# Loading k's last rows ahead of q's, and taking k's norms before q's, at the start of an attention-and-feed-forward kernel

## The chip, the cores and the metric

The kernel runs on one core of a Trainium2 chip. The metric is the device time of that core in microseconds (us), lower is better. Before the change it was 720.33 us (median of 3 runs, 720.29 to 720.56).

Each run gives two figures. *Time* is the metric. *Span* is the stretch from the first to the last thing that the profile of that run shows. The time is 1.7 to 2.9 us longer than the span, and that difference wanders from run to run without the kernel having a part in it. Where tenths of a microsecond matter, the span is the sharper of the two, and I give both. Each run also has a mean granted TensorE clock, 1.000 being full speed.

## The reference

```python
# B, N, C = 4, 6080, 256
qn = q / (norm(q, axis=1) + 1e-6)           # norms over the 6080 rows, one per channel
kn = k / (norm(k, axis=1) + 1e-6)
s  = kn.transpose(0, 2, 1) @ qn / tau       # 256 x 256 scores per batch, tau = 1
a  = softmax(s, axis=-1)
x  = (v @ a).reshape(B * N, C)
h  = relu(x @ w_in)                         # 256 -> 2048
out = (s_moe * h * h + b_moe) @ w_out       # 2048 -> 256
```

Nothing of the feed-forward part can begin before the first batch's softmax is known, and that needs the sums of squares over all 6080 rows of k and q. So the last rows to arrive stand at the head of a chain: square, norm, root, scaling, exp, fold into w_in, first product.

## The kernel before

The names: PE is TensorE (matmuls), ACT is ScalarE, DVE is VectorE, POOL is GpSimd, which issues the loads. Batch 0 is read in 13 pieces. The first eleven hold 4 rows per partition, the last two 2 rows per partition, on 128 and on 96 partitions. In the text, q11 and q12 are q's last two pieces, k11 and k12 those of k.

```python
def load(self, c):
    ...
    for i, src in enumerate((k, q)):                       # k's piece, then q's piece
        ...
        po(nc.gpsimd.dma_start(out=t[:np_, i, :jc, :], in_=rows))

for c in range(NDIRECT, len(g0.chunks)):
    g0.load(c)                                             # ... k11, q11, k12, q12, then w_in, v
```

`po` keeps the order of the program on an engine. The scores of a piece are the `mm` matmuls; `keep_busy` issues matmuls whose result nobody reads, to keep PE's clock up.

```python
for c in range(NCH0):
    ops = g0.norm_ops(c)              # square of k on ACT, of q on DVE, folds on DVE
    if c >= NCH0 - 3:
        g0.add_norms()                # matmuls with ones: sums of squares of earlier pieces
    for j in range(g0.chunks[c][2]):
        g0.mm(c, j)                   # scores
    fill = FILL.get(c - NCH0, 0)      # 4 for the piece before the last two, 1 behind piece 11
    if fill:
        keep_busy(fill, ...)
    for f in ops:
        f()

fin = g0.finish_ops()
fin[1]()   # norms of k and q together on PE, one root on ACT
fin[2]()   # + eps and reciprocal on DVE, of k and q
fin[3]()   # scores times 1/|k| on DVE
fin[4]()   # ready(Exp): loads ACT's table for exp, with a tiny exp called warm
keep_busy(4, w_in16[:, 0, :P], w_in16[:, 0, :NW])
fin[5]()   # turn: four transposes of the scores on PE
transpose_v(0)
for f in fin[6:12]:
    f()    # exps, sums, folds into w_in
```

After that the main loop runs in steps: a step has one first product (`mm1`, two matmuls of 512 columns), one relu on ACT every second step, and second products. Those of group 0 are placed by one line:

```python
if s == gp * FT + PLAG[gp] + (mp * 3 // 2 if gp == 0 else mp):     # FT = 16, PLAG[0] = 11
    plain_mm2(gp, mp)
```

## Time and profile before

| | before |
|---|---|
| time, median | 720.33 us |
| span of the profiled run | 718.5 us |
| PE busy | 97% of the span |
| q's last rows land | 34.36 us |
| first exp on ACT | 37.36 us |
| group 1's sums S begin on DVE | 68.73 us |
| PE without a stall from | 76 us |

How to read it: PE is full from 76 us to 703, and its work after that is the same in both kernels. So whatever the change gains or loses is decided before 76 us. The lines that carry this are shown and explained in the prediction.

### The profile page before, as it was taken

The numbers are of one execution on the slowest core, as the hardware profiler recorded it, in microseconds if no ns is written. First come the engines' busy times: TensorE is split into PE (matmuls) and PEld (weight loads), VectorE is DVE, ScalarE is ACT, GpSimd is POOL, SyncE is SP. The second block draws the span as 40 slices with busy tenths as digits, with TensorE's granted clock in tenths as the row PEclk, the third lists the DMA queues.
The fourth block names the chain that finished last, engine by engine and source line by source line (L and its number), as shares of the span: only waits on it lengthen the run. The fifth ranks groups of instructions, "written<-read, shape, count | busy, mean of one in ns | idle before, by whom it ended". The sixth has DMA issues, their size and how long they took to land.

```text
span 718.5 us, 17642 instructions
## 1 busy us (share of the span) xinstructions
PE 699.4 (97%) x7481; PEld 505.0 (70%) x7481; DVE 625.9 (87%) x879; ACT 544.5 (76%) x588; POOL 109.8 (15%) x189
## 2 busy tenths in 40 slices
PE   4799999999999999999999999999999999999998
PEld 3556777776677777777677777777668777777777
DVE  4779999998889999999888899999887888888886
ACT  4489877887777777788777777778877777777875
POOL 4532332201201222111110222110000000000000
PEclk9999999999999999999999999999999999999999
DMA  9999999547565979443973777844423333321202
GB/s 237 207 259 148 172 166 149 110 103 134 103 105 120 153 133 144 105 96 75 152 155 63 139 136 125 154 93 83 105 65 75 92 71 74 97 59 46 83 30 75
DMA packets 89791, 84.27 MB, mean 117 GB/s; under 512 B 59664, under 2 KB 64848, under 8 KB 89712
## 3 DMA queue, kind: packets, MB, share of 16 engines
q0 software_dynamic: 26064, 43.40, 37.7%
q1 hardware_dynamic: 63072, 38.43, 21.5%
q8 instruction: 59, 0.97, 0.5%
q10 hardware_dynamic: 576, 1.31, 0.5%
q14 instruction: 20, 0.16, 0.1%
HBM read 78.91 MB, written 24.90 MB: 144 GB/s over the span
## 4 chain that ended last, share of the span: by engine, by line
PE 92%; DMA 4%; ACT 1%; DVE 1%; POOL 0%; issue 0%; ACTq 0%; POOLq 0%
PE h_ps L605 45%; PE o_ps L773 40%; PE s_ps L142 4%; PE wa_ps L309 2%; DMA qk<-in_q_dram 2%; DMA qk<-in_k_dram 1%; DMA w_in<-in_moe_w_in_dram 1%; ACT r L615 1%; PE o_ps L651 0%; POOL qk L126 0%; PE o_ps L677 0%; ACT g L626 0%; PE idle_ps L442 0%; DVE o_sb L633 0%; DVE sq L162 0%
## 5 line engine op out<-in xcount | busy, mean ns | idle before, releaser
L615 ACT ACTIVATE r<-h_ps 128x1024 f16<-128x1024 f32 (+1 forms) x384 | 387.6, 1013 | 146.9 <-PE h_ps L605 145.0
L605 PE MATMUL h_ps<-vT,wa 128*128 128x512 f16 (+7 forms) x1632 | 451.9, 364 | 0.6 <-ACT r L615 0.4
L773 PEld LDWEIGHTS <-S 128*128 128x128 f16 x2944 | 197.9, 98 | 85.1 <-DVE S L699 0.4
L773 PEld LDWEIGHTS <-g 128*128 128x128 f16 x2208 | 155.0, 98 | 74.1
L628 DVE TENSOR_TENSOR g<-r 128x2048 f16<-128x2048 f16 (+2 forms) x150 | 174.7, 1165 | 15.1 <-ACT r L615 14.9
L773 PE MATMUL o_ps<-T,S 128*128 128x128 f16 x2208 | 183.2, 219 | 0.3 <-DVE S L699 0.2
L605 PEld LDWEIGHTS <-wa 128*128 128x128 f16 x1632 | 136.0, 98 | 21.4 <-issue 1.0
L773 PE MATMUL o_ps<-w_out,g 128*128 128x128 f16 x1472 | 134.2, 219 | 0.3 <-DVE u L633 0.3
L633 DVE SCALAR_TENSOR_TENSOR o_sb<-o_ps,s_out,u 128x256 f32<-128x256 f32 x138 | 66.4, 481 | 47.6 <-PE o_ps L773 45.1
L626 ACT ACTIVATE g<-r 128x1024 f16<-128x1024 f16 (+1 forms) x97 | 100.4, 1035 | 0.2
L142 PE MATMUL s_ps<-qk 128*128 128x256 f16 (+1 forms) x384 | 70.0, 283 | 14.0 <-ACT qk L133 8.7
L361 POOL DMA_DIRECT2D v<-in_v_dram x48 | 31.3, 656 | 263.0 <-DMA vT<-v 199.5
L633 DVE SCALAR_TENSOR_TENSOR u<-o_ps,s_out,rowconst 128x256 f32<-128x256 f32 x138 | 65.9, 478 | 0.0
L773 PE MATMUL o_ps<-w_out,S 128*128 128x128 f16 x736 | 63.4, 219 | 0.0
L773 PE MATMUL o_ps<-N,g 128*128 128x128 f16 x736 | 63.4, 219 | 0.0
L188 POOL DMA_DIRECT2D f<-f x30 | 26.3, 877 | 225.8 <-DVE f L178 167.0
L165 ACT ACTIVATE sq<-qk 128x1024 f16<-128x1024 f16 (+3 forms) x49 | 50.4, 1033 | 10.3 <-DMA qk<-in_k_dram 6.3
L701 DVE TENSOR_TENSOR S<-S,g 128x2048 f16<-128x2048 f16 (+1 forms) x47 | 56.4, 1201 | 1.3
L699 DVE TENSOR_TENSOR S<-g 128x2048 f16<-128x2048 f16 (+1 forms) x47 | 56.0, 1192 | 0.0
L705 DVE TENSOR_TENSOR S<-g,S 128x2048 f16<-128x2048 f16 x46 | 55.9, 1216 | 0.0
L703 DVE TENSOR_TENSOR S<-g 128x2048 f16<-128x2048 f16 x46 | 55.9, 1215 | 0.0
L142 PEld LDWEIGHTS <-qk 128*128 128x128 f16 (+1 forms) x384 | 32.9, 101 | 19.8 <-DVE qk L132 8.1
(75 smaller groups left out, 324.3 us busy)
## 6 DMA issues: line engine op xcount, KB each, us to landing
out_dram<-o_sb SPq DMA_DIRECT2D x46, 512.0 KB, 3.0
v<-in_v_dram POOLq DMA_DIRECT2D x47, 256.0 KB, 4.7
qk<-in_k_dram POOLq DMA_DIRECT2D x42, 256.0 KB, 6.0
qk<-in_q_dram POOLq DMA_DIRECT2D x42, 256.0 KB, 7.2
f<-f POOLq DMA_DIRECT2D x30, 128.0 KB, 3.0
vT<-v SPq DMA_TRANSPOSE x182, 3.2
w<-in_moe_w_out_dram POOLq DMA_DIRECT2D x4, 512.0 KB, 11.4
raw<-in_q_dram ACTq DMA_DIRECT2D x2, 512.0 KB, 6.6
```

The lines of the kernel that those rows point to most:

```text
L142: po(nc.tensor.matmul(self.s_ps[:, ch, :], kc[:np_, j, ts(ch, P)], qc[:np_, j, :], start=(c == 0 and j == 0 and ch == 0), stop=(c == len(s ...
L165: po(nc.scalar.activation(out=st["sq"][:np_, 1, js, :], in_=kc[:np_, js, :], func=AF.Square))
L605: po(nc.tensor.matmul(dst, wa[:, ci, ts(m, P)], src, start=(ci == 0), stop=(ci == CH - 1), skip_group_check=True))
L615: po(nc.scalar.activation(out=r16[:, :, i % 2, :n], in_=h_tiles.pop((g, i))[:, :, :n], func=AF.Relu))
L626: po(nc.scalar.activation(out=dst, in_=src, func=AF.Square))
L628: po(nc.vector.tensor_mul(dst, src, src))
L633: po(nc.vector.scalar_tensor_tensor(out=dst, in0=src, scalar=s_out, op0=ALU.mult, in1=add, op1=ALU.add))
L699: po(nc.vector.tensor_add(T[1], A21, A22))
L701: po(nc.vector.tensor_sub(T[2], T[1], A11))
L703: po(nc.vector.tensor_sub(T[3], A11, A21))
L705: po(nc.vector.tensor_sub(T[4], A12, T[2]))
L773: po(nc.tensor.matmul(st[name][:, j, :], a()[:, i, ts(j, P)], w[:, i, :], start=first, stop=last, skip_group_check=True))
```

## The change

The intent: k's last rows are asked for ahead of q's, so that all that depends on k alone (its norms, their roots, their reciprocals, the scaling of the scores) can be done ahead of q's norms. Besides that, three of the four padding matmuls ahead of the transposes go, and group 0's second products are placed at 4/3 of a step instead of 3/2. The diff cut to its core:

```diff
-    for c in range(NDIRECT, len(g0.chunks)):
+    for c in range(NDIRECT, len(g0.chunks) - 2):
         g0.load(c)
+    for parts in ((0,), (1,)):                       # k11, k12, then q11, q12
+        for c in range(len(g0.chunks) - 2, len(g0.chunks)):
+            g0.load(c, parts)
...
+    NFILL = 1
...
+    fin = g0.finish_ops()
     for c in range(NCH0):
         ops = g0.norm_ops(c)
         if c >= NCH0 - 3:
             g0.add_norms()
+        if c == NCH0 - 1:
+            for f in ops:
+                f()
+            fin[0]()                                 # norms of k, and their root
         for j in range(g0.chunks[c][2]):
             g0.mm(c, j)
...
-    fin[1](); fin[2](); fin[3](); fin[4]()           # (four lines in the original)
-    keep_busy(4, w_in16[:, 0, :P], w_in16[:, 0, :NW])
-    fin[5]()
+    for f in fin[1:6]:      # norms of q, ready(Exp), recip of k, scale, recip of q
+        f()
+    keep_busy(NFILL, w_in16[:, 0, :P], w_in16[:, 0, :NW])
+    fin[6]()                # turn
...
-                if s == gp * FT + PLAG[gp] + (mp * 3 // 2 if gp == 0 else mp):
+                if s == gp * FT + PLAG[gp] + (mp * 4 // 3 if gp == 0 else mp):
```

The rest of the diff (cut here) splits the norm tile, the root and the reciprocal into one for k and one for q in batch 0, and leaves the later batches as they were.

More of the change, by code (lines that the diff above doesn't have):

```diff
@@ L114, in __init__, with load @@
             self.tiles = {}
-            self.rows, self.n_ps = [], None
-        def load(self, c):
+            self.raw, self.rows, self.n_ps = {}, ([], []), [None, None]
+        def load(self, c, parts=(0, 1)):
             at, np_, jc = self.chunks[c]
-            t = qk_pool.tile([P, 2, JC, C], FP16, tag="qk", name="qk")
+            if 0 in parts:
+                self.raw[c] = qk_pool.tile([P, 2, JC, C], FP16, tag="qk", name="qk")
+            t = self.raw[c]
             direct = self.b == 0 and c < NDIRECT
-            for i, src in enumerate((k, q)):
+            for i in parts:
+                src = (k, q)[i]
                 rows = src[self.b, at : at + np_ * jc, :].rearrange("(p j) c -> p j c", j=jc)
@@ L181, in f @@
                     if last and (self.b == 0 or c == 0 or c == len(self.chunks) - 1):
-                        self.rows.append((st["f", half], np_, 1))
+                        for rows in self.rows:
+                            rows.append((st["f", half], np_, 1))
                 return f
             def into_first():
-                dst, src = self.rows[0][0][:np_], st["f", 1][:np_]
+                dst, src = self.rows[0][0][0][:np_], st["f", 1][:np_]
                 po(nc.gpsimd.dma_start(out=dst, in_=src, accum_op=ALU.add))
             def unfolded():
-                self.rows.append((st["sq"], np_, jc))
+                for rows in self.rows:
+                    rows.append((st["sq"], np_, jc))
             ops = []
@@ L202, in norm_ops, with add_norms @@
             return ops + [into_first] if self.b > 0 and 0 < c < len(self.chunks) - 1 else ops
-        def add_norms(self, last=False):
-            first = self.n_ps is None
-            if first and self.b == 0:
-                self.n_ps = ps_o.tile([P, 2, C], FP32, tag="o_ps", name="n_ps")[
-                    :, 0, : 2 * CH].rearrange("p (a c) -> p a c", a=2)
-            elif first:
-                self.n_ps = x_tile[0][:, 1, : 2 * CH].rearrange("p (a c) -> p a c", a=2)
-            todo = [(t, np_, j, a, ch) for t, np_, jc in self.rows for j in range(jc)
-                    for a in range(2) for ch in range(CH)]
-            self.rows = []
-            for i, (t, np_, j, a, ch) in enumerate(todo):
-                po(nc.tensor.matmul(self.n_ps[:, a, ch : ch + 1], t[:np_, a, j, ts(ch, P)],
-                                    ones16[:np_, 0:1], start=(first and i == 0 and self.b == 0),
-                                    stop=(last and i == len(todo) - 1), skip_group_check=True))
+        def add_norms(self, arrays=(0, 1), last=False):
+            if self.b > 0:
+                self.n_all = x_tile[0][:, 1, : 2 * CH].rearrange("p (a c) -> p a c", a=2)
+                self.n_ps = [self.n_all[:, 0], self.n_all[:, 1]]
+            for a in arrays:
+                first = self.n_ps[a] is None
+                if first:
+                    self.n_ps[a] = ps_o.tile([P, 2, C], FP32, tag="o_ps", name="n_ps")[:, 0, :CH]
+                todo = [(t, np_, j, ch) for t, np_, jc in self.rows[a] for j in range(jc)
+                        for ch in range(CH)]
+                self.rows[a].clear()
+                for i, (t, np_, j, ch) in enumerate(todo):
+                    po(nc.tensor.matmul(self.n_ps[a][:, ch : ch + 1], t[:np_, a, j, ts(ch, P)],
+                                        ones16[:np_, 0:1], start=(first and i == 0),
+                                        stop=(last and i == len(todo) - 1),
+                                        skip_group_check=True))
@@ L221, in finish_ops, with norms @@
         def finish_ops(self):
             st = {}
-            def norms():
-                self.add_norms(last=True)
-                nrm = sm_pool.tile([P, 2, CH], FP32, tag="nrm", name="nrm")
-                po(nc.scalar.activation(out=nrm, in_=self.n_ps, func=AF.Sqrt))
-                st["nrm"] = nrm
-            def recip():
-                nrm = st["nrm"]
+            def norms(a=None):
+                if "r" not in st:
+                    st["nrm"] = sm_pool.tile([P, 2, CH], FP32, tag="nrm", name="nrm")
+                    st["r"] = sm_pool.tile([P, 2, CH], FP32, tag="rnrm", name="rnrm")
+                if a is None:
+                    self.add_norms(last=True)
+                    po(nc.scalar.activation(out=st["nrm"], in_=self.n_all, func=AF.Sqrt))
+                else:
+                    self.add_norms((a,), last=True)
+                    po(nc.scalar.activation(out=st["nrm"][:, a], in_=self.n_ps[a], func=AF.Sqrt))
@@ L233, in recip @@
+            def recip(a=None):
+                own = slice(0, 2) if a is None else slice(a, a + 1)
+                nrm, r = st["nrm"][:, own], st["r"][:, own]
                 po(nc.vector.tensor_scalar_add(out=nrm, in0=nrm, scalar1=EPS))
-                st["r"] = sm_pool.tile([P, 2, CH], FP32, tag="rnrm", name="rnrm")
-                po(nc.vector.reciprocal(out=st["r"], in_=nrm))
-                if inv_tau != 1.0:
+                po(nc.vector.reciprocal(out=r, in_=nrm))
+                if inv_tau != 1.0 and a != 1:
@@ L337, in finish_ops @@
                       for m in range(CH)]
-            front = [lambda: ready(AF.Sqrt), norms, recip]
             if self.b == 0:
-                front += [scale, lambda: ready(AF.Exp), turn]
+                front = [lambda: norms(1), lambda: norms(0), lambda: ready(AF.Exp),
+                         lambda: recip(1), scale, lambda: recip(0), turn]
             else:
+                front = [lambda: ready(AF.Sqrt), norms, recip]
                 front += [lambda: ready(AF.Exp), lambda: split("hi"), lambda: split("lo"), join]
@@ L453 @@
                       g0.tiles[c][0][:, :2, :].rearrange("p j c -> p (j c)"))
-        for f in ops:
-            f()
-    fin = g0.finish_ops()
-    fin[1]()
-    fin[2]()
-    fin[3]()
-    fin[4]()
-    keep_busy(4, w_in16[:, 0, :P], w_in16[:, 0, :NW])
-    fin[5]()
+        if c < NCH0 - 1:
+            for f in ops:
+                f()
+    for f in fin[1:6]:
+        f()
+    keep_busy(NFILL, w_in16[:, 0, :P], w_in16[:, 0, :NW])
+    fin[6]()
     transpose_v(0)
-    for f in fin[6:12]:
+    for f in fin[7:13]:
         f()
@@ L519 @@
     FOLDS = (0, 0, 3, 4, 7, 8)
-    for i, f in enumerate(fin[12:]):
+    for i, f in enumerate(fin[13:]):
         at_step(FOLDS[i], f)
```

## The prediction

> **What bounds the kernel now.** I read the page first. PE is busy 97% and the slices of part 2 show it below 9 tenths only in the first two, 0 to 36 us, and in the last, so what a change at the front can save is time in which PE starts late or still stalls.
>
> ```profile
> PE 699.4 (97%) x7481; PEld 505.0 (70%) x7481; DVE 625.9 (87%) x879; ACT 544.5 (76%) x588; POOL 109.8 (15%) x189
> PE   4799999999999999999999999999999999999998
> PE 92%; DMA 4%; ACT 1%; DVE 1%; POOL 0%; issue 0%; ACTq 0%; POOLq 0%
> ```
>
> The chain of waits that ended last (third line) is DMA for its first 4% and PE after that; from 76.6 to 703 us it holds only matmuls. So the gain is decided before 77 us, in two places. First, the timeline between the arrival of the last rows of q and the first exp (columns: start us, duration us, engine, line, what; brackets: idle before and releaser):
>
> ```profile
> 34.36 0.42 DVE L162 TENSOR_TENSOR sq<-qk 96x512 f16<-96x512 f16 x1 [1.22 <-DMA qk<-in_q_dram]
> 34.84 0.35 PE L217 MATMUL n_ps<-ones,sq 96*128 96x1 f16 x8
> 35.23 0.17 ACT L228 ACTIVATE nrm<-n_ps 128x4 f32<-128x4 f32 x1 [1.86 <-PE n_ps L217]
> 35.42 1.28 ACT L277 ACT_TABLE_LOAD   x1
> 35.43 0.19 DVE L233 TENSOR_SCALAR nrm<-nrm 128x4 f32<-128x4 f32 x1 [0.65 <-ACT nrm L228]
> 35.46 1.04 PE L442 MATMUL idle_ps<-w_in 128*128 128x512 f16 x4 [0.27 <-DMA w_in<-in_moe_w_in_dram]
> 35.95 0.88 DVE L243 TENSOR_SCALAR sm_s<-s_ps,rnrm 128x256 f32<-128x256 f32 x2
> 36.58 0.74 PE L272 MATMUL t_ps<-ident,sm_s 128*128 128x128 f32 x4
> 36.71 0.20 ACT L277 ACTIVATE warm<-ones 128x1 f32<-128x1 f32 x1
> 37.36 0.84 ACT L282 ACTIVATE eT<-t_ps,rnrm 128x256 f16<-128x256 f32 x2 [0.44 <-PE t_ps L272]
> ```
>
> Two branches meet at the exp. DVE and PE: square of q, norms, root, add and reciprocal, scale, four transposes, ending 37.32. ACT: root, table load, warm, ending 36.91. The first is later by 0.44 us, the idle time in the last line. The padding matmuls (L442) also hold PE till 36.50.
>
> Second, the chain of waits in order of time, 49 to 75 us (start, duration, what). After 37.4 it is PE without a gap to 49.5; then it is not:
>
> ```profile
> 49.57 1.02 ACT r L615
> ...
> 58.02 0.92 ACT r L615
> ...
> 65.67 0.04 DVE g L628
> 65.70 1.11 issue
> 66.81 0.68 DVE sq L162
> 67.49 1.32 DVE o_sb L633 x2
> 68.82 1.14 DVE S L699
> ...
> 74.27 0.41 DVE u L633
> ```
>
> From 49.6 to 59.0 ACT's relus and casts hold it, from 65.7 to 74.7 DVE does: group 0's two evacuations (L633) stand just ahead of the sums S that group 1's products wait for, although DVE sat idle 1.00 us waiting for the relu that its square at 65.67 reads.
>
> **What the Trainium skill says.** "ScalarE: Activation LUTs", section "What ACT_TABLE_LOAD costs", gives 1283 ns for a table load and 1380 ns for a drain with it. The trace agrees with the load (1.28 us); no such drain shows, the root ending at 35.40 and the load starting at 35.42. "TensorE: Matmul & The Clock Gate", section "Back-to-back issue gap", gives N/2.4 + 2.5 ns, 216 ns at N = 512; the chain's pieces of two such matmuls are 0.43 us, so I count a step's pair at 0.43, four of 256 columns at 0.43 and two at 0.22, and ignore the 0.38 us latencies in the busy sums. The same page, section "What's actually happening", puts the clock down after an idle window of about 3.4 us; dropping three padding matmuls (0.65 us) leaves no such gap, and the granted clock is 1.00 throughout the front, so I charge nothing. "DMA: Bandwidth & Descriptors", section "Two DMAs through the same engine are not ordered", says that nothing orders transfers across the 16 engines: the landing of one transfer does not follow from bytes alone. The trace shows it: q's last 96 KB landed 1.6 us after k's (ACT's square of k 32.74, DVE's of q 34.36), where 205 GB/s would take 0.48.
>
> **The change part by part.**
>
> *Loading order.* k's last two pieces (128 and 96 KB) go ahead of q's. Bytes before q's last row are the same, and the queue moves a steady 200 to 212 GB/s in every microsecond from 30 to 37, issued 8 us ahead. So q's last rows still land near 34.36; k's last come about 0.6 us earlier (128 KB at 205 GB/s) and q's last but one about 0.5 later.
>
> *k's norms and root early.* 12 small matmuls and a root of 0.17 us move into the wait before 34.36. Cost: one more root, 0.2 us, in ACT's idle 1.86 us. PE's risk: after q's last but one piece it has 4 score matmuls (0.43), one filler (0.22), 8 norm matmuls and k's 4 (0.4), about 1.1 us; if that piece lands at 33.3, PE is ready at 34.4, just in time, or up to 0.2 late.
>
> *DVE branch after.* Square ends 34.78; add and reciprocal of k and the scale's start took 0.52 from 35.43 to 35.95, so the scale starts at about 34.76 + 0.52 = 35.3 instead of 35.95. The transposes ended 1.37 after the scale's start (37.32 - 35.95), so 36.65. Only one filler is left before them, from 35.46 to 35.68, so PE is free. q's add and reciprocal follow the scale: 36.15 + 0.45 = 36.6.
>
> *ACT branch after.* q's norms are 4 matmuls instead of 8, which takes about 0.1 off: root at 35.1 to 35.2, load and warm 1.49 later. From root's start to warm's end was 36.91 - 35.23 = 1.68, so exp can start at 36.8 to 36.9. This branch is now the later one. Exp moves from 37.36 to about 36.9: **0.45 us**, not the 0.65 of the DVE branch. Behind exp PE is contiguous to 49.5 and no transfer lands within 0.4 us of its use (w_in's second piece, 8.0 us after 29.91, lands at 37.9 and is read at 39.8), so it carries.
>
> *Second products of group 0 at 4/3 instead of 3/2 of a step.* The sixteen (0.43 us each) now end at step 31 instead of 33. Placing steps on the timeline (mm1 of step 25 at 58.00, of 26 at 58.99), PE stalled 0.10 before step 18, 0.30 before 24 and 0.56 before 26, about 1.0 us, while ACT ran without a gap. Before step 26 there are now 12 second products instead of 10, so 0.87 us of PE work goes into those stalls. By step 31, 15 instead of 14: the relu of that step was waiting for PE. I get PE's step 31 at 63.1 to 63.6 instead of 63.98 to 64.6, 1.0 us earlier with the first gain, or less where it waits for ACT.
>
> *DVE.* Group 0's evacuations now stand at step 31, before the square of step 32, and fill the idle 1.00 us. DVE: the last instruction ahead of them, that of rowconst (0.48 us from 64.18, so to 64.66), ends at 64.2 with the shift of 0.45, then evacuations 1.32, square 1.14, square of k's rows 0.6: S starts at 67.3 instead of 68.8. So DVE's chain is ahead by up to 1.45 and PE by 1.1 plus its own waits (0.20 at 70.0, 0.27 at 71.8, 0.33 at 74.7). The later branch decides; ideally 1.4 us in all at 74.7. I take 0.8 for this part rather than 0.95, because ACT is saturated in 50.5 to 61.7 and again from 67.9, and its relus, which free the two h buffers, may hold PE.
>
> *Sum.* 0.45 + 0.80 = 1.25 us off 720.33: **719.1 us**.
>
> **The rivals.** (1) *The table load hides the front gain*: if q's rows land later, or PE reaches its last norms late, ACT's branch ends at 37.1 to 37.3 and the first gain is 0.1 to 0.2. For it: 1.68 us of ACT follows q's root whatever k does. Against: ACT had 0.44 to spare. Time 719.4 if the rest holds. (2) *The second products only move PE work about*: ACT's relus bound steps 14 to 26, extra matmuls delay mm1 and so relu, DVE stays full and hands nothing on. For it: ACT has no idle 50.5 to 61.7. Against: the stalls are on PE's side, and mm1 reached ACT about 0.4 us before ACT took it at step 19 and more at 21 and 23. Time 719.9. (3) *Everything lands*: all PE stalls before 75 us go, about 1.0 + 0.8, with 0.45: 718.1. (4) *A wait takes its place*: w_out's cast ends at 51.53, and the second product that reads it moves from step 17 to 16, which comes at about 51.1 (cast then ends 51.1 too); or four small pieces reordered make the last q land 0.5 late. Time 720.3 to 720.8.
>
> **Range and chances.** Rivals 1 and 2 together leave 720.1, rival 3 leaves 718.1; repeats of the kernel lie within 0.3 us. Range 718.4 to 720.0. A change of 2% is 14.4 us; all of the front until PE is full is 38 us of which DMA transfers are most, so neither side has more than half a per cent.
>
> **What would show it.** Right: exp starts 0.3 to 0.6 earlier, with ACT's warm as the last releaser rather than the transposes; k's root before 34.4, k's reciprocal before q's root ends; no stall of 0.5 before step 26; L633's evacuations of group 0 ahead of the 128x2048 square and L699 about 1.4 us earlier; the chain then all PE from about 73. Wrong: q's last rows landing away from 34.4; exp still waiting for the transposes; DVE idle again before its square; PE stalls moved later instead of removed, so that the lead at 50 us is larger than the one at 100 us.

## The result, and the profile after

The changed kernel takes **720.08 us** in the median of 6 runs (718.96 to 721.11), against 720.35 us for 6 runs of the kernel before (720.24 to 720.56). The ratio is 0.9996, with a 95% interval of 0.9983 to 1.0009. A ratio here is always the mean time of one kernel's fast runs over that of the other's of the same rounds, so it isn't quite the ratio of the medians. No difference is proved, and the predicted 719.1 isn't reached; the median lies just above the range of 718.4 to 720.0. The remarkable thing is the spread: 2.15 us, where the kernel before had 0.32.

The page of the changed kernel (the run profiled first, span 718.6 us, granted clock 0.998) has almost the same shares, first of the engines, then of the chain that ended last:

```profile
PE 700.1 (97%) x7478; PEld 505.9 (70%) x7478; DVE 626.1 (87%) x881; ACT 544.6 (76%) x589; POOL 110.1 (15%) x189
PE 93%; DMA 4%; DVE 1%; ACT 1%; POOL 0%; issue 0%; POOLq 0%; DVEq 0%; ACTq 0%
```

The timeline of its front, with the same columns as before (start, duration, engine, line, what; in brackets the idle time before and what ended it):

```profile
34.16 0.76 DVE L166 TENSOR_TENSOR sq<-qk 128x512 f16<-128x512 f16 x2 [1.35 <-DMA qk<-in_q_dram]
34.18 0.60 PE L146 MATMUL s_ps<-qk 128*128 128x256 f16 x4 [1.05 <-DMA qk<-in_q_dram]
...
35.13 0.60 PE L146 MATMUL s_ps<-qk 96*128 96x256 f16 x4
35.30 0.17 ACT L243 ACTIVATE nrm<-n_ps 128x2 f32<-128x2 f32 x1 [2.29 <-PE n_ps L224]
...
35.84 0.17 ACT L243 ACTIVATE nrm<-n_ps 128x2 f32<-128x2 f32 x1 [0.36 <-PE n_ps L224]
...
36.62 1.09 PE L286 MATMUL t_ps<-ident,sm_s 128*128 128x128 f32 x4 [0.57 <-DVE sm_s L257]
...
37.33 0.20 ACT L291 ACTIVATE warm<-ones 128x1 f32<-128x1 f32 x1
37.74 0.84 ACT L296 ACTIVATE eT<-t_ps,rnrm 128x256 f16<-128x256 f32 x2 [0.21 <-PE t_ps L286]
```

Two things went otherwise than intended.

First, q11 landed only at 34.16, so late that its square and that of q12 run back to back (the "x2" of the first line). PE had waited 1.05 us for it, and then the work of both pieces stood in a queue: scores of q11 at 34.18, a filler, norms, scores of q12 at 35.13. k's root, which should have been done in the wait, came at 35.30, because k's norms stand behind the scores of q11 on PE. q's root came at 35.84, where it was at 35.23 before; with load and warm behind it, ACT was ready 0.6 us later than before.

Second, the four transposes took 1.09 us instead of 0.74, which put the exp another 0.2 us behind ACT. In the windows view (start:end, length, then busy time of PE, PEld, DVE, ACT, POOL, then PE's granted clock, DMA share, GB/s):

```profile
19.36:22.77 3.41, 1.97 (x13) 1.08 (x12) 3.17 (x6) 1.61 (x2) 1.14 (x3) 1.00 1.12 210
33.03:36.44 3.41, 1.97 (x31) 1.38 (x27) 1.55 (x6) 0.75 (x3) 2.06 (x4) 1.00 1.20 207
36.50:39.70 3.20, 3.01 (x21) 2.53 (x22) 1.38 (x5) 2.10 (x5) 1.55 (x3) 0.50 1.14 213
```

The clock record in this trace puts PE at full speed from 15.95 us, at half from 36.43 and at full again from 39.84. These times are 6 and 1 times 3.41 us apart. In the step of 3.41 us before the fall PE was busy for only some 1.97. But the first line shows an earlier step of the same grid with the same 1.97, and behind that one the clock stayed at full. So PE's busy time alone doesn't tell when the clock falls.

So at the first product the kernel was behind: it began at 40.13, against 39.31 before. And yet the span is the same to 0.1 us. The other half shows in the chain of waits in order of time (start, duration, what) from 53 to 70 us:

```profile
53.54 1.02 ACT r L637
...
57.37 0.92 ACT r L637
...
65.72 1.41 DVE o_sb L655 x2
67.13 1.13 DVE g L650
68.26 0.60 DVE sq L166
68.86 1.15 DVE S L721
```

The stretch that ACT holds now ends at 58.3 instead of 59.0, though everything began 0.8 later. Group 0's evacuations (o_sb) stand ahead of the square (g) now, DVE's idle 1.00 us before that square is gone, and S begins at 68.8 as in the kernel before. The back had made up for what the front lost.

### The profile page after: what moved, and what is told of

Read it like the earlier page. It is cut to its first block, busy times and chain, and to the rows that moved or that the text cites. A ratio compares the mean times of both kernels' runs of the same rounds, so it can differ in the third digit from the quotient of the medians.

```text
span 718.6 us, 17639 instructions
## 1 busy us (share of the span) xinstructions
PE 700.1 (97%) x7478; PEld 505.9 (70%) x7478; DVE 626.1 (87%) x881; ACT 544.6 (76%) x589; POOL 110.1 (15%) x189
## 4 chain that ended last, share of the span: by engine, by line
PE 93%; DMA 4%; DVE 1%; ACT 1%; POOL 0%; issue 0%; POOLq 0%; DVEq 0%; ACTq 0%
PE h_ps L627 45%; PE o_ps L795 40%; PE s_ps L146 4%; DMA qk<-in_k_dram 3%; PE wa_ps L323 2%; DMA qk<-in_q_dram 1%; PE o_ps L699 1%; PE o_ps L673 0%; ACT r L637 0%; POOL qk L130 0%; DVE o_sb L655 0%; DVE S L723 0%; DVE sq L166 0%; DVE S L721 0%; DVE g L650 0%
```

## The experiments

Eleven kernels were run, the first ten on one chip with shared runs of the kernel before, the eleventh on another chip. All gave a correct result. The shared runs of before on the first chip: their spans are 718.3 to 718.7 in all but one (719.9), with a median of 718.5 and a mean time of 720.6.

| kernel | loads, padding, second products | time, median | spans of its runs | granted clock below 1.000 | first exp (profiled run) |
|---|---|---|---|---|---|
| before, 11 runs | k,q each; 4; 3/2 | 720.5 | 718.3 to 718.7, one 719.9 | one 0.999 | 37.36 |
| after, first 6 runs | k,k,q,q; 1; 4/3 | 720.08 | 717.2 to 719.3 | two 0.998 | 37.74 |
| e1_back_only | k,q each; 4; 4/3 | 720.29 | 717.6 to 718.0 | one 0.999 | 37.67 |
| e2_front_only | k,k,q,q; 1; 3/2 | 720.12 | 718.1 to 718.2, one 719.4 | two 0.999, one 0.998 (the 719.4) | 36.87 |
| e3_old_loads | k,q each; 1; 4/3 | 719.65 | 717.4 to 718.9 | 0.998, 0.999 (the longest two) | 36.95 |
| e4_fill_wait | k,k,q,q; 4 more ahead of q11, 1; 4/3 | 720.15 | 717.9 to 718.1 | one 0.999 | 37.52 |
| e5_old_loads_fill | k,q each; 2 + 3; 4/3 | 719.61 | 717.5 to 718.0 | none | 37.29 |
| e6_new_loads_fill | k,k,q,q; 2 + 3; 4/3 | 719.70 | 717.6 to 718.1 | one 0.999 | 37.00 |
| e7_before_one_fill | k,q each; 1; 3/2 | 721.19 | 718.5 to 719.8 | 0.998, 0.998, 0.997 | 37.37 |
| e8_q_swapped | k,k, then q12, q11; 2 + 3; 4/3 | 720.57 | 718.1 to 718.5 | one 0.999 | 37.90 |
| e9_k_first_on_pe | as e6 with 3 more ahead of q11, k's norms first on PE | 719.42 | 717.4 to 717.6 | one 0.999 | 37.10 |
| e10_after_again | k,k,q,q; 1; 4/3 (the change itself) | 719.87 | 717.2 to 719.4 | one 0.999 (the 719.4) | 36.70 |
| e11_k_recip_first | as e9, k's reciprocal first on DVE | 719.35 | 717.4 to 717.9 | one 0.999 | 36.77 |

One step of 3.41 us at half speed makes a mean of 0.998 over 718 us (1 - 0.5 * 3.41 / 718 = 0.9976). Both falls on record lasted such a step (below), and a value of 0.999 is too high for that. The profile of e4, at 0.999, shows where it can come from instead: its clock is full until 717.13 us and at half for the 0.9 us left, when PE has nothing more to do. So a long run at 0.999 isn't explained by a fall of the clock at the front, and neither is the run of before with 719.9 us at 1.000; their cause is open.

My first theory, from the one profile that I had: the front loses 0.4 to 0.9 us in every run, through the order of loads and through the clock, and the back gains 0.9. The rival: the back gains nothing of its own, it only absorbs a late front.

### e1_back_only: the second products alone

```diff
-  (mp * 3 // 2 if gp == 0 else mp)
+  (mp * 4 // 3 if gp == 0 else mp)          # on the kernel before
```

> The kernel before with one line changed: group 0's second products at 4/3 of a step. Theory (front loses, back gains): the profile of the changed kernel is 0.9 us late at 40 us and level again at 75 us, so the back part alone is worth about 0.9 us: 719.4, exp still at 37.4. Rival (the back part only absorbs a late front, because whatever comes late finds the same ACT and DVE waits shorter): 720.2 or more, no gain by itself.

Measured: the spans are 717.6 to 718.0 (median 717.8), 0.7 under before. The median time of 720.29 didn't show it, since these five runs happened to have 2.4 us outside the span in the mean, where those of before had 2.0; the ratio of times is 0.9993 (0.9981 to 1.0006). On the span, the theory of a gain by the back itself holds and the rival falls; on the time, nothing is proved. DVE's timeline shows the mechanism:

```profile
65.14 1.41 DVE L633 SCALAR_TENSOR_TENSOR o_sb<-o_ps,s_out,rowconst 128x512 f32<-128x512 f32 x2
68.20 1.22 DVE L699 TENSOR_TENSOR S<-g 128x2048 f16<-128x2048 f16 x1
```

From the first exp (37.67) to S it is 30.53 us; in the kernel before it is 68.73 - 37.36 = 31.37. From the first exp to the end of the span it is 718.0 - 37.67 = 680.33 against 718.5 - 37.36 = 681.14. So the back is worth 0.81 us.

### e2_front_only: the loads and norms alone

```diff
-  (mp * 4 // 3 if gp == 0 else mp)
+  (mp * 3 // 2 if gp == 0 else mp)          # on the changed kernel
```

> The changed kernel with group 0's second products back at 3/2 of a step, so the loads and norms alone. Theory (front loses): exp at 37.4 to 37.8, time 720.4 to 721.4, slower than before by the front's loss, and the runs at a granted clock below 1.00 the slowest. Rival (the back absorbs): about 720.1, like the whole change.

Measured: 720.12, and in the profile the first exp at 36.87, half a microsecond *earlier* than before. My theory fell: the front does not lose in every run. Counted from the start of DVE's square of q's last piece, the exp comes 2.36 us later here (36.87 - 34.51) and 3.00 us in the kernel before (37.36 - 34.36), so the front gains 0.64 us at the exp. In this run q11 had landed by 33.17, PE did its work in the wait, k's root came at 34.55 and q's at 35.27. The spans are 718.1 to 718.2 in four runs, 0.3 under before, and 719.4 in the one whose clock was 0.998. From the first exp to the end it is 681.33 us, 0.19 more than in the kernel before, so not all of the gain at the exp carries. In this trace DVE begins to scale its first folded piece 0.85 us after the folds' matmuls begin (38.68 after 37.83; before 0.64, 38.98 after 38.34), PE waits for it in the first product, and ACT's stretch begins 0.31 earlier than before (49.26 against 49.57), not 0.5. What made DVE wait longer there isn't shown. So there are good and bad executions of the same program, and the profile of the changed kernel that I had been explaining was one of the bad ones.

The theory became: the front gains some 0.5 us at the exp if q11 comes in time; it loses if q11 comes together with q12; and, apart from that, the clock falls in some of the runs because too little padding is left.

### e3_old_loads: the order of loads undone

```diff
-    for c in range(NDIRECT, len(g0.chunks) - 2):
+    for c in range(NDIRECT, len(g0.chunks)):
         g0.load(c)
-    for parts in ((0,), (1,)):
-        for c in range(len(g0.chunks) - 2, len(g0.chunks)):
-            g0.load(c, parts)
```

> The changed kernel with the last loads in the order of before (k, q of each piece), norms of k still ahead. Theory of the landing (q's last two pieces came together at 34.2 because the last but one was put behind k's): q's last but one piece lands by 32.8 again, q's last near 34.4, q's root at 35.1 to 35.2, exp at 36.8 to 36.9, granted clock 1.00, time 718.9 to 719.2. Rival of the clock (fewer padding matmuls alone are the loss): PE's transposes still take over 1.0 us for four in some runs, granted clock 0.998, exp at 37.2 or later, time 719.8 to 720.4.

Measured: the profiled run went nearly as expected (q's root at 35.35, exp at 36.95, each 0.1 to 0.2 late with q12's landing; span 717.4, time 719.22). The median of 719.65 did not, and two of the five runs had a clock of 0.998 and 0.999 with spans of 718.4 and 718.9. The first of these is a fall of the clock, the second, as said above, isn't explained. So the fall of the clock is not tied to the new order of loads. Neither theory alone was enough.

### e4_fill_wait: more padding in the wait for q11

```diff
-    FILL = {..., -4: 4, -3: 4, -2: 1}
+    FILL = {..., -4: 4, -3: 8, -2: 1}
```

> The changed kernel with 8 instead of 4 padding matmuls (0.86 us more) behind the chunk before q's last two pieces, where PE waited 1.05 us. Theory of the clock as a second loss: granted clock 1.00 in every run, four transposes back at 0.74 us and the eight folds of 256 columns near 1.03 instead of 1.45, but q's root still near 35.8 and exp near 37.5, time about 719.5 and little spread. Rival (the drop of the clock has another cause, such as the padding left out after q): clock still 0.998 in some runs, time 720.1 as before with a spread of 2 us.

Measured: transposes back at 0.74 us, q's root at 35.76, exp at 37.52, spans within 0.2 us of each other; one run at 0.999, the profiled one, whose windows from 28 to 48 us are all at 1.00. The time, 720.15, missed the expected 719.5. There is a confusion in it that I had not foreseen: q11 had landed by 32.97 here, and the extra padding itself kept PE from its scores until 34.10. It shows that PE's queue costs the same whether it is late by the load or by padding.

### e7_before_one_fill: padding taken from the kernel before

```diff
-    keep_busy(4, w_in16[:, 0, :P], w_in16[:, 0, :NW])
+    keep_busy(1, w_in16[:, 0, :P], w_in16[:, 0, :NW])    # on the kernel before
```

> The kernel before with one padding matmul instead of four ahead of the turn. Theory: exp unmoved at 37.3 to 37.4 (the scale sets it), but the clock falls to half in some of the runs (0.998 or 0.999), which then take 0.5 to 0.9 us longer; span 718.4 otherwise. Rival (padding there is worth nothing for the clock, it only held PE): 1.000 in all, 718.3 to 718.5.

Measured: 721.19, three of its four runs at a clock of 0.997 or 0.998 with spans of 719.4, 719.4 and 719.8, and one at 1.000 with 718.5. The exp did not move (37.37). This is the cleanest of the results on the clock: with three padding matmuls less, 0.65 us of work, the span is 0.9 to 1.3 us longer in three runs of four. (On the time, four runs prove no difference: ratio 1.0006, 0.9992 to 1.0019.) Its windows view, in the stretch before the fall and in the one after:

```profile
33.90:37.31 3.41, 2.18 (x29) 1.52 (x28) 1.64 (x5) 2.29 (x4) 2.50 (x4) 1.00 1.18 209
37.40:40.70 3.30, 3.12 (x21) 2.04 (x19) 1.68 (x4) 1.76 (x4) 0.74 (x2) 0.50 1.11 242
```

PE was busy 2.18 us of 3.41 and the clock fell. In the kernel before, the same stretch has 2.67 us of PE and nothing fell:

```profile
33.90:37.31 3.41, 2.67 (x27) 1.51 (x25) 1.67 (x5) 1.66 (x3) 2.26 (x4) 1.00 1.18 210
```

Here too the busy time doesn't decide alone: in e7's own trace the step from 20.30 to 23.71 has 1.60 us of PE, and the clock stayed at full. The clock's changes stand at 16.88, 37.36 and 40.78 us, again 6 and 1 steps apart, 0.9 us later than in the changed kernel's profile. So where the grid lies differs from run to run.

### e5_old_loads_fill and e6_new_loads_fill: padding put where PE waits anyway

```diff
-    NFILL = 1
+    NFILL = 2
...
     transpose_v(0)
+    keep_busy(3, w_in16[:, 0, :P], w_in16[:, 0, :NW])     # while ACT does the exps
```

e5 is this on e3, e6 is this on the changed kernel.

> The loads in the order of before, norms of k ahead, and five padding matmuls instead of one behind the front: two ahead of the turn, three behind v's transposes, where PE waits for the exps. Theory (two losses: late rows of q, and half a clock for 3.2 us when PE does too little): granted clock 1.000 in all runs (0.998 and 0.999 in two of five without the padding), exp at 36.7 to 37.0, span 717.2 to 717.7 with a spread under 0.6, about 1.0 under before. Rival (the clock falls with this order whatever PE does): 0.998 or 0.999 in some run again, spans up to 718.9.

> The changed kernel with the same five padding matmuls. Theory: granted clock 1.000 in all runs, so no span over 718.3; spans from 717.2 to 718.2 by the landing of q's last but one piece (exp at 36.9 where it lands by 33.3, 37.4 or later where it lands after 34). Rival (the new order of loads loses by itself in every run): all spans 717.9 or more.

Measured: e5 was at 1.000 in all runs. e6 had one 0.999, with a span of 717.9, which is not a long one. No run of either is over 718.1, and both are at 719.6 to 719.7. That agrees with the clock as a loss of its own, removed by padding that costs nothing. Over all runs the count is clear: with one padding matmul behind q's last piece (the changed kernel, e2, e3, e7, e10) 7 of 25 runs have a clock of 0.998 or less; with four or five there (before, e1, e5, e6, e8, e9, e11) none of the 50 whose clock is on record. (e4, with one there and eight ahead of q11, has none in 5.) The exp of e5 missed: 37.29 instead of 36.7 to 37.0, and so did its spans, 717.5 to 718.0 instead of 717.2 to 717.7. Its profile shows why. There *k12* landed late, at 34.19, and k's root came at 35.16. So the old order of loads has the same weak point in another place: in both orders it is the third of the four small pieces that sometimes comes more than a microsecond late (e8 shows the same with q12 in third place). In the kernel before that did no harm, since k's norms waited for q's anyway. e6's q11 came in time: q's root at 35.41, exp at 37.00.

### e8_q_swapped: the late landing made sure

```diff
-        for c in range(len(g0.chunks) - 2, len(g0.chunks)):
+        for c in range(len(g0.chunks) - 2, len(g0.chunks))[:: 1 if parts == (0,) else -1]:
             g0.load(c, parts)                 # on e6: k11, k12, q12, q11
```

> As e6_new_loads_fill, with q's two last pieces loaded in reverse, so that the one whose matmuls stand first always lands last, near 34.4. Theory (a late last but one piece of q puts all of both pieces' work behind it: 0.43 + 0.22 + about 0.3 + 0.43 + norms): q's root at 35.9 to 36.1, exp at 37.5 to 37.8 in the profile, spans 718.0 to 718.3 at a granted clock of 1.000, little spread. Rival (the landing does not matter, the work behind it overlaps): exp at 36.9 to 37.1, spans as e6_new_loads_fill's best.

Measured, in the timeline:

```profile
34.33 0.76 DVE L166 TENSOR_TENSOR sq<-qk 128x512 f16<-128x512 f16 x2 [1.32 <-DMA qk<-in_q_dram]
...
36.01 0.17 ACT L243 ACTIVATE nrm<-n_ps 128x2 f32<-128x2 f32 x1 [0.36 <-PE n_ps L224]
...
37.90 0.84 ACT L296 ACTIVATE eT<-t_ps,rnrm 128x256 f16<-128x256 f32 x2 [0.20 <-PE t_ps L286]
```

q's root came as expected, the spans (718.1 to 718.5) and the exp 0.1 to 0.2 over what I had said. ACT's warm ends 3.36 us behind the late piece (37.69 - 34.33), as it did in the changed kernel's bad profile (37.53 - 34.16 = 3.37), here at full clock. In both the exp came 0.2 us after that, but for different reasons: there the transposes were slow, here an addition of DVE ahead of the scaling took 0.50 us instead of 0.17, which I can't explain. Against e6, whose only difference is the order of two loads, the spans are 0.4 us longer in the mean (718.27 against 717.84). So the late landing of q11 alone takes the front's gain away, and more.

### e9_k_first_on_pe: nothing of k behind q on PE

```diff
+    a, b2 = g0.norm_ops(NCH0 - 2), g0.norm_ops(NCH0 - 1)
+    g0.add_norms()
+    for f in a[:2] + b2[:2]:          # squares of k11 and k12
+        f()
+    fin[0]()                          # norms of k on PE, root on ACT
+    keep_busy(3, ...)                 # in the wait for q11
+    for f in a[2:]:                   # square of q11
+        f()
+    fin[3]()                          # + eps and reciprocal of k on DVE
+    for f in b2[2:]:                  # square of q12
+        f()
+    for c in (NCH0 - 2, NCH0 - 1):    # scores of q11, then of q12, no filler between
+        for j in range(g0.chunks[c][2]):
+            g0.mm(c, j)
+    fin[1](); fin[2](); fin[4](); fin[5]()
```

(Added lines only, cut; the two and three padding matmuls of e6 stay.)

> As e6_new_loads_fill (new order of loads, five padding matmuls), and on PE both of k's last norms stand ahead of the score matmuls that wait for q's last two pieces, q's norms of both behind these, with three padding matmuls in the wait. Theory (a late q costs because the work of both pieces and k's norms queue behind it): k's root by 33.6 whatever q does, exp 2.3 to 2.6 us after q's last piece lands even where its last but one is late (3.56 in the changed kernel's profile, 2.36 in e6_new_loads_fill), granted clock 1.000 (0.999 at most), spans 717.3 to 717.8. Rival (the order on PE does not matter, the table load decides alone): spans as e6_new_loads_fill, 717.6 to 718.1.

Measured: **719.42 us** with six runs between 719.17 and 719.49, spans 717.4 to 717.6, ratio to the kernel before 0.9983 (0.9970 to 0.9995). It is the only one of eleven here whose interval excludes 1; all six runs lie below the fastest of the 11 of before (720.10). q11 was late in its profile, and it did not matter:

```profile
33.34 0.17 ACT L242 ACTIVATE nrm<-n_ps 128x2 f32<-128x2 f32 x1 [0.36 <-PE n_ps L223]
...
34.14 0.43 DVE L166 TENSOR_TENSOR sq<-qk 128x512 f16<-128x512 f16 x1 [1.36 <-DMA qk<-in_q_dram]
...
37.10 0.82 ACT L295 ACTIVATE eT<-t_ps,rnrm 128x256 f16<-128x256 f32 x2
```

k's root begins 0.8 us before q11's square does, and the exp comes 2.96 us after it instead of 3.58. I had expected 2.3 to 2.6, so that part missed.

### e10_after_again: the changed kernel once more

No edit.

> The changed kernel unchanged, on the same chip as the others. Theory: spans between 717.2 and 719.4, some runs at 0.997 or 0.998 and these the longest, 718.5 or more; median span 718.0 to 718.4, so 0.1 to 0.5 under before. Rival (the losses of the first six runs were accidents of that chip): all at 1.000 and 717.2 to 717.9.

Measured: median 719.87, spans 717.2, 717.3, 718.1, 718.3 and 719.4, the last at a clock of 0.999, the others at 1.000. The profiled run was one of the good ones, at 719.08 us:

```profile
34.34 0.42 DVE L166 TENSOR_TENSOR sq<-qk 96x512 f16<-96x512 f16 x1 [0.95 <-DMA qk<-in_q_dram]
...
35.11 0.17 ACT L243 ACTIVATE nrm<-n_ps 128x2 f32<-128x2 f32 x1 [0.58 <-PE n_ps L224]
...
36.70 0.82 ACT L296 ACTIVATE eT<-t_ps,rnrm 128x256 f16<-128x256 f32 x2
```

No run fell to 0.998, where I had expected some. This is the execution that the prediction describes, almost to the number: q's root at 35.1, exp at 36.7 behind ACT's warm, 719.1 us. The eleven runs of the changed kernel (6 and 5) fall into three groups: four spans of 717.2 to 717.4 and four of 717.9 to 718.3, all eight at 1.000, and three of 718.6 to 719.4 at 0.998 or 0.999. Of these runs only two have a profile in this document, so that the middle group is the one with a late q11 is an inference from e8's spans of 718.1 to 718.5, not shown.

### e11_k_recip_first: one more order on DVE

```diff
-    for f in a[2:]:
-        f()
     fin[3]()
-    for f in b2[2:]:
+    for f in a[2:] + b2[2:]:
         f()                           # on e9
```

> As e9_k_first_on_pe, with k's add and reciprocal on DVE ahead of both squares of q's last pieces instead of between them. In that profile q's last square began at 34.76, behind k's reciprocal, 0.62 after the one before it, so q's root at 35.51 and exp at 37.10. Theory (that order cost about 0.3 where q's pieces come together): the two squares back to back, q's root 1.0 to 1.2 us after the first of them where they come together, exp about 2.7 us after it, spans 717.1 to 717.5, time about 719.2. Rival (PE's score matmuls of the last piece set q's norms, not DVE): exp within 0.1 of 2.96 us after the first square, spans 717.4 to 717.6 as before.

Measured: 719.35 against 720.33 on that chip, spans 717.4 to 717.9, exp 2.87 us after the first square. That lies inside what the rival had, and the spans are not shorter than e9's. The DMA view puts q11's landing 9.1 us after its issue, at 33.88, so this too was a late one. There is nothing further in this order that I could show.

## Why the prediction was right or wrong

The predicted 719.1 us was wrong for the kernel as it usually runs (720.08, and 719.87 in the second five) and right for about one execution in three of those seen. Point by point:

- **The bound, and the two branches that meet at the exp: right.** With q11 in time, the exp waits for ACT's table load and warm, not for the transposes: 36.70 in e10, 36.87 in e2, against the predicted 36.9. From q12's square to the exp it is 2.36 us in e2, e3, e6 and e10, where it was 3.00, so the gain at the exp was 0.64 and not the predicted 0.45. That this gain "carries" was too much: e2 alone is 0.3 shorter at the end.
- **The second products at 4/3 and DVE's order: right, in mechanism and in size.** I took 0.80 us. From the first exp to the end, the back alone saves 0.81 (e1 against before), and 681.33 - (717.3 - 36.70) = 0.73 us with the new front (e2 against e10). In e10 S begins at 67.51 where I had 67.3. What held it there was PE: the evacuations began at 64.45, behind the last second products, where I had 64.2. I had cut 0.95 to 0.80 for ACT's relus, so that the sum fits so closely is in part luck.
- **The padding, of which I wrote "so I charge nothing": the first step that failed.** I had reasoned that taking out 0.65 us of padding leaves no idle gap of about 3.4 us. None was needed: the clock went to half for 3.41 us behind a step in which PE was busy for 1.97 or 2.18 us. That costs 0.9 to 1.3 us in e7, and it happened in two of the first six runs. What in a step makes the clock fall stays open, since steps with as little PE work, at 17 to 24 us, held it.
- **"q's last but one about 0.5 later": the second step that failed.** In the first profile q11 landed at 34.16, at least 1.4 us behind its old place (its square began at 32.72 before), together with q12. I had named PE's queue as the risk and allowed "up to 0.2 late"; q's root was 0.6 later than before. The term was mis-sized by the landing, and so was rival 1, which has the same mechanism with 37.1 to 37.3 for the end of ACT's branch, where it was 37.53. Rival 4 saw danger in the reordered pieces, but for the last one, and that came in time (34.33 in the trace, 34.34 before). The queue was also less steady than I had it: 195 to 217 GB/s in the single microseconds from 30 to 37, not 200 to 212. By weight this second step is likely the first: 8 of 11 runs of the change had full clock, four of them at 717.9 to 718.3. That a late q11 alone puts a run there is shown by e8; that it did so in those four is inferred.
- **The range, with "repeats of the kernel lie within 0.3 us": it was drawn from the steadiness of the kernel before.** The steadiness was a property of that schedule: its k norms waited for q anyway, and its padding held the clock. The changed schedule bares both, and its runs spread over 2.1 us. The range should have been wider for that, on the slow side.
- **Less than 2% either way: right.**

Where the gain went, then: 0.7 to 0.8 from the back alone (e1), 0.3 at the end from the front alone when q11 comes in time and the clock holds (e2), and 1.2 from both together in e10 (717.3 against 718.5). When q11 is late, q's root is 0.6 to 0.8 us later than before (35.84 and 36.01 against 35.23) and the front is a loss; when the clock falls, more is lost: 0.9 to 1.3 in e7, less in the changed kernel's profile (from the exp to the end 680.86, against 680.58 in e4 and 680.60 in e8 at full clock). What makes the third small piece in the queue late in some executions stays open. It happened to k12 in three of five profiles with the old order of loads (e1, e5, e7), and in the new order to q11 in the first profile, in e9 and in e11 and to q12 in e8, but not in e2, e4, e6 and e10.

A version that beats the kernel before, and is steadier than the change, is e9: the change with k's norms truly first on PE and eight padding matmuls in PE's waits (three ahead of q11, two ahead of the transposes, three behind v's).

## What to carry to other kernels

When an order is changed so that one branch gets ahead, look on *every* engine for what still stands in front of that branch: here k's rows were loaded first, but on PE k's norms stayed behind scores that wait for q, and the gain hung on the landing of one transfer. Matmuls that only keep the clock up are part of the schedule; after taking some out, look at the granted clock of several runs, since neither PE's longest gap nor its busy share foretold the fall here, and put padding where PE waits anyway. And one profile is one execution: take a few of them before explaining a difference of half a microsecond, and compare spans as well as times.

## What the Trainium skill lacked or had wrong

- "TensorE: Matmul & The Clock Gate", section "What's actually happening", lets the clock fall "after ≥1 idle window (~3.4µs)". In these runs it fell behind steps of 3.41 us in which PE was busy for 1.97 us (changed kernel) and 2.18 us (e7), and it held behind one with 1.97 us in the same changed kernel's trace. What makes a window an idle one, the page doesn't say. The half clock agrees with it (0.50). So does its "free-running" window: the clock's changes lie 6 and 1 times 3.41 us apart in both traces, from 15.95 us in one and from 16.88 in the other.
- "ScalarE: Activation LUTs", section "What ACT_TABLE_LOAD costs", counts 1380 ns of drain with each load. Here the root before the load ended at 35.40, the load began at 35.42, took 1.28 us, and the first function of the new set began at 36.71: no drain is seen.
- "DMA: Bandwidth & Descriptors" has no figure for how far the landing of one small transfer wanders in a full queue. Here a piece of 96 or 128 KB, third of four, landed 7.5 to 7.8 us after its issue in six profiles and 8.8 to 9.3 us in seven (7.8 in e10, 9.3 in the changed kernel), while the whole queue moved 191 to 217 GB/s.
